# A linear-attention and sine-feed-forward kernel: mixed rows kept in order until the store, the head's copies dealt out anew, decay rates on another queue

## The chip, the cores and the metric

The kernel runs on one core of a Trainium2 chip. A core has five engines with queues of their own: TensorE (PE, matrix products from SBUF into PSUM banks), VectorE (DVE), ScalarE (ACT), GpSimd (POOL) and SyncE (SP, which here only issues transfers). Transfers between memory and SBUF run on 16 DMA engines; SP, ACT and POOL each have a queue to them. Engines run by themselves and wait for each other by semaphores. The metric is the device time of one execution in microseconds.

## The reference, cut to what matters

Stage one is linear attention with decay, for 4 batches, 8 heads, 768 positions, 64 channels; stage two is a feed-forward layer over the 3072 tokens of 512 channels:

```
for each block b of 64 positions:
    out[b] = ((q_b k_b^T) * lam^(i-j), lower triangle) v_b  +  (q_b * lam^(i+1)) state
    state  = lam^64 * state + (k_b * lam^(63-j))^T v_b
x   = out, tokens x 512
h   = x @ w_in                       # 512 -> 2048
g   = h + sin(alpha*h)^2 / (alpha + 1e-9)
res = g @ w_out                      # 2048 -> 512
```

## The kernel before, in words

**Tiling.** The kernel uses blocks of 128 positions, 24 in all (six to a batch), and gives tokens to stage two in six groups of 512 (four blocks). q and k are scaled by powers of the decay rate, cast to bf16 (`qk2`), transposed (`qkT`); a product of the two (S, L635) times a mask gives `Sm` (L646, DVE); `Sm` times v plus the earlier blocks' state times q gives the output piece O (L708, L721, L730), and k times v adds to the state Z (L671, copied to `Zd` or `Zc`). O lies in PSUM with channels on partitions and tokens along the columns, and is copied as columns of `xT` (L740). Stage two: unit A multiplies `w1` with `xT` (L779 for 512 columns, L813 for 256), ACT takes the sine (L789, L823), ACT or POOL the square (L793, L794, L827, L828), DVE makes `gT` (L796, L831); unit B multiplies `gT` with `w2` (L844), ACT copies it to `osb` (L857) and a transfer stores 128 tokens (L859).

**Mixed rows.** Blocks 0 to 3 are loaded in a shape that makes long runs: partition p of the q tile holds tokens 4p to 4p+3 (L357). After the transposes, column x of slot t is token 4x+t. The copy to `xT` (L740) puts the tokens back in order: it reads "t x" and writes "x t", so each write steps over `nq` columns, 4 in blocks 0 to 3 and 2 later, where pairs of blocks are loaded in the same way.

**Order.** A planner (`_Plan`) gets every operation with an engine, or a choice of engines, and a duration. It goes through time, gives each engine what is ready first (PE looks 40 operations ahead, SP takes its own in the order of the program), models the transfers, and writes each engine's instructions out in that order with the waits needed. Durations in it decide order and the choice of engine. `ported` marks operations that the planner keeps from running beside each other on DVE and POOL. Gaps of PE in the head are filled with matmuls on a constant tile (L935).

**The head.** Before stage two starts, SP issues the loads of q, k and v of blocks 0 to 3 and of the first quarter of `w1`; ACT requests the decay rates (`lam`, L426) and `alphaT` (L427). The rates go through Ln and Exp on ACT to the factors `Lq`, `Lp`, `Lk`. POOL issues the other weight loads (L346 from L397 and L418) between its own operations. The load of block 4's q waits until the third quarter of `w1` has landed (L901). The stores of the first 512 tokens are kept back and given to SP in one go (L960 to L962); in SP's order they stand behind the loads of blocks 10 and 11 and ahead of those of block 12. All other stores are issued by ACT, but the last one.

Of the kernel before, what the change touches and what calls it, by code (L numbers as in the profile page):

```python
# [6 lines left out]
ACTF = mybir.ActivationFunctionType  # L7
# [236 lines left out]
def bass_lightning_attn__then__act_snake_kernel(  # L244
# [31 lines left out]
    RO = 4  # L276
    RX = 3
    RU = 4
    QD = ((0, 0), (1, 0))

    es = contextlib.ExitStack()
    with es:
# [51 lines left out]
        def _(_unused_eng):  # L334
# [7 lines left out]
            def bank(i):  # L342
                return ("bank", i)
# [79 lines left out]
                )  # L423

            last = {}
            load(lam_bc[:, :], bass.AP(lam.tensor, 0, [[0, 128], [1, H]]), "lam", 0.1, "lam", "ACT", runs=1)  # L426
            load(alphaT[:, :], bass.AP(moe_alpha.tensor, 0, [[128, NM], [1, 128]]), "alphaT", 0.1, "alphaT", "ACT", lat=4.9, runs=1)  # L427
            load_q(0)
            load_kv(0, "k")
# [27 lines left out]
            for i in range(2):  # L457
                op("POOL", lambda e, i=i: e.memset(Zd[i][:, :, :], 0.0), 0.5, writes=[("Zd", i, 0), ("Zd", i, 1), "select"])

            op("ACT", lambda e: e.activation(lnlam[:, :], lam_bc[:, :], ACTF.Ln), 1.5, ["lam"], ["lnlam"])  # L460
            lnlam_b = bass.AP(lnlam, 0, [[H, 128], [0, 2 * NB + 4], [1, H]])
            op("DVE", lambda e: e.tensor_tensor(lnL[:, :, :], E_f[:, :, :], lnlam_b, ALU.mult), 0.2,
               ["E_f", "lnlam"], ["lnL"])
            op("ACT", lambda e: e.activation(Lq[:, NB:NB + 4, :], lnL[:, 2 * NB:2 * NB + 4, :], ACTF.Exp), 0.3,
               ["lnL"], ["Lq4"])
            op("ACT", lambda e: e.activation(Lp[:, :, :], lnL[:, 0:NP, :], ACTF.Exp, scale=-1.0), 0.2,
               ["lnL"], ["Lp"])
            op("ACT", lambda e: e.activation(Lk[:, :, :], lnL[:, NB:2 * NB, :], ACTF.Exp, scale=-1.0), 0.3,
               ["lnL"], ["Lk"])
            op("ACT", lambda e: e.activation(Lq[:, 0:NB, :], lnL[:, 0:NB, :], ACTF.Exp), 0.3, ["lnL"], ["Lq"])  # L470
            op("ACT", lambda e: e.activation(warm[:, :], lnlam[:, 0:1], ACTF.Sin, scale=0.0), 1.5,
               ["lnlam", "Lk", "Lq", "Lq4", "Lp"], ["warm"])

            op("PE", lambda e: e.transpose(ps[4][:, 0:NM], alphaT[:, :], identf[0:NM, 0:NM]), 0.3,
               ["alphaT", "identf"], [bank(4)])
            op("DVE", lambda e: e.tensor_copy(alpha[:, :], ps[4][:, 0:NM]), 0.2, [bank(4)], ["alpha"])
            op("DVE", lambda e: e.tensor_scalar_add(aeps[:, :], alpha[:, :], 1e-9), 0.2, ["alpha"], ["aeps"])
            op("DVE", lambda e: e.reciprocal(rinv[:, :], aeps[:, :]), 0.2, ["aeps"], ["rinv"])

            def QE(s, a):  # L480
                return "DVE" if (s, a) in QD else "POOL"

            def ported(o):
                o.port = True
                return o

            def scale_block(s):
                n, jl, j = s % NB, s % RL, s % R2
                lk = bass.AP(Lk, n * H, [[NB * H, 128], [1, H], [0, D]])
                jq = s // 2 % (RL // 2)  # L490
                if s == 0:
                    for a in range(2):
                        for t in (0, 2):
                            (op(QE(a, t),
                               lambda e, a=a, t=t: e.tensor_tensor(
                                   qk2[:, t:t + 2, 4 * a:4 * a + 4, :],
                                   bass.AP(q32, (a * H * 2 + t) * D,
                                           [[RL * H * D, 128], [D, 2], [4 * D, 4], [1, D]]),
                                   bass.AP(Lq, (NB + t) * H + 4 * a, [[(NB + 4) * H, 128], [H, 2], [1, 4], [0, D]]),
                                   ALU.mult),  # L500
                               1.05 if QE(a, t) == "POOL" else 0.9,
                               [("q32", a, 0), ("q32", a, 1), "Lq4"], [("q2", t, a), ("q2", t + 1, a)]))
                for a in range(2) if s % 2 == 0 and s > 2 else ():
                    ported(op("POOL",
                       lambda e, a=a: e.tensor_tensor(  # L505
                           qk2[:, j:j + 2, 4 * a:4 * a + 4, :],
                           q32[:, jq, 4 * a:4 * a + 4, :, :].rearrange("p h t d -> p t h d"),
                           bass.AP(Lq, n * H + 4 * a, [[(NB + 4) * H, 128], [H, 2], [1, 4], [0, D]]), ALU.mult),
                       1.05, [("q32", jq, a), "Lq"], [("q2", j, a), ("q2", j + 1, a)]))
                if s < NP:  # L510
                    for a in range(2) if s % 2 == 0 else ():
                        eng, dur = (("DVE", 0.9) if a == 0 else ("POOL", 1.05)) if s == 0 else ("POOL", 1.05)
                        (op(eng, lambda e, a=a: e.tensor_tensor(  # L513
                            qk2[:, j:j + 2, H + 4 * a:H + 4 * a + 4, :],
                            pair32(k32, jl, a).rearrange("p h t d -> p t h d"),
                            bass.AP(Lp, n * H + 4 * a, [[NP * H, 128], [H, 2], [1, 4], [0, D]]), ALU.mult),
                           dur, [("k32", jl + a), "Lp"], [("k2", j, a), ("k2", j + 1, a)]))
                    for a in range(2) if s % 2 == 0 else ():
                        op("ACT" if s + a == 0 else "POOL", lambda e, a=a: (e.copy if e is nc.scalar else e.tensor_copy)(
                            v2[:, j:j + 2, 4 * a:4 * a + 4, :],  # L520
                            pair32(v32, jl, a).rearrange("p h t d -> p t h d")), 0.62,
                           [("v32", jl + a)], [("v2", j, a), ("v2", j + 1, a)])
                    return
                ported(op("POOL",
                   lambda e: e.tensor_tensor(qk2[:, j, H:2 * H, :], block32(k32, jl), lk, ALU.mult), 1.05,  # L525
                   [("k32", jl), "Lk"], [("k2", j, 0), ("k2", j, 1)]))
                op((("ACT", 0.62, 0.0), ("POOL", 1.05, 0.3)) if s > 11 else "ACT",
                   lambda e: (e.copy if e is nc.scalar else e.tensor_copy)(v2[:, j, :, :], block32(v32, jl)), 0.62,  # L528
                   [("v32", jl)], [("v2", j, 0), ("v2", j, 1)])
# [94 lines left out]
            def part_S(s, b0, b1):  # L624
                jt = s % RT
                jq, nq, u = queries(s)

                def mm(e):
                    ins = None
                    for jp in range(4):  # L630
                        for h in range(2):
                            r = slice(64 * h, 64 * h + 64)
                            for c in range(2) if s < NP else (None,):
                                x = slice(0, 128) if c is None else slice(64 * c, 64 * c + 64)
                                ins = e.matmul(  # L635
                                    ps[(b0, b1)[h]][x, 128 * jp:128 * (jp + 1)].rearrange("p (t x) -> p t x", t=nq),
                                    qkT[r, jt, 4 + jp, x],
                                    qkT[r, jq:jq + nq, jp, u if c is None else queries(s // 2 * 2 + c)[2]],
                                )
                    return ins  # L640

                assert b1 == b0 + 1
                mi, js = (s % 2, s % 4) if s < NP else (2, s % 2)

                def then():
                    op("DVE", lambda e: e.tensor_tensor(  # L646
                        Sm[js][:, :, :],
                        banks[:, 512 * b0:512 * b0 + 1024].rearrange("p (c i) -> p c i", i=128),
                        bass.AP(mask[mi], 0, [[128, 128], [0, 8], [1, 128]]), ALU.mult), 1.25, [bank(b0), bank(b1), ("mask", mi)], [("Sm", js)])

                return mm, 0.33, [("qT", jq + t) for t in range(nq)] + [("kT", jt)], [bank(b0), bank(b1)], then

            def diag(s):
                return s < NP - 1 or s >= SD
# [37 lines left out]
            def part_O(s, ob, ob2=None):  # L692
# [43 lines left out]
                    return ins  # L736

                def then():
                  for eng, a0, a1, dur in ((("ACT", 0, 2, 0.45), ("DVE", 2, 4, 0.4)) if ob2 is not None else (("ACT" if s < 2 else (("ACT", 0.73, 0.4), ("DVE", 0.7, 0.0)), 0, 4, 0.74),)):
                    op(eng, lambda e, a0=a0, a1=a1: (e.copy if e is nc.scalar else e.tensor_copy)(  # L740
                        xT[c % RX][:, a0:a1, BL * i4:BL * (i4 + 1)].rearrange("p a (x t) -> p a t x", t=nq),
                        ps[obs[a0 // 2]][:, 128 * a0:128 * a1].rearrange("p (a t x) -> p a t x", a=a1 - a0, t=nq)), dur,
                       [bank(obs[a0 // 2])], [("xT", c % RX, i4, a) for a in range(a0, a1)])

# [92 lines left out]
            def unit_B(c, s4, mq, ob, lo=0, hi=DM, out_eng="ACT"):  # L837
# [18 lines left out]
                row = TCH * c + 128 * s4  # L856
                op("ACT", lambda e: e.copy(osb[jo][:, w], ps[ob][:, w]), 0.6, [bank(ob)], [("osb", jo)])  # L857
                def store(eng):
                    op(eng, lambda e: e.dma_start(out[row:row + 128, w], osb[jo][:, w]), 0.75,  # L859
                       [("osb", jo)], [], dma=f"out{jo}", issue=0.3, runs=8)  # L860

                if out_eng is None:
# [31 lines left out]
            piece_O(3, 2, 5)  # L894
            load_w1_first()
            cast_w1_first()
            for i in range(1, 4):
                load_w1(i, [last["v32", 1]])
            for i in range(4):
# [136 lines left out]
```

## Time and profile before

| | us |
|---|---|
| runs | 221.79, 222.25, 227.55 (median 222.25) |
| profiled execution | 221.06 |
| its span | 219.2 |
| PE busy | 207.6 (95%) |
| ACT, DVE, POOL busy | 157.2, 123.0, 96.0 |
| PE's first matmul of stage two (L813) | 20.58 |
| last load of q, k, v landed | about 122 |

Times within the profile count from the start of the span; 1.86 us of the profiled execution lie outside it. "Busy" is the time in which an engine has an instruction; PE's matmuls overlap, so a busy PE need not be at its peak. The slices of the page are 5.48 us each, a digit is a share in tenths. A line such as "ACT u L827" is an operation of ACT that writes tile `u` at line 827 of the kernel; "DMA q<-in_q_dram" is a transfer from its issue to its landing; "SPq" is SP at issuing.

### The profile page before, as it was taken

The numbers are of one execution on the slowest core, as the hardware profiler recorded it, in microseconds if no ns is written. First come the engines' busy times: TensorE is split into PE (matmuls) and PEld (weight loads), VectorE is DVE, ScalarE is ACT, GpSimd is POOL, SyncE is SP. The second block draws the span as 40 slices with busy tenths as digits, with TensorE's granted clock in tenths as the row PEclk, the third lists the DMA queues.
The fourth block names the chain that finished last, engine by engine and source line by source line (L and its number), as shares of the span: only waits on it lengthen the run. The fifth ranks groups of instructions, "written<-read, shape, count | busy, mean of one in ns | idle before, by whom it ended". The sixth has DMA issues, their size and how long they took to land.

```text
span 219.2 us, 4238 instructions
## 1 busy us (share of the span) xinstructions
PE 207.6 (95%) x1714; PEld 112.2 (51%) x1739; DVE 123.0 (56%) x185; ACT 157.2 (72%) x279; POOL 96.0 (44%) x110
## 2 busy tenths in 40 slices
PE   7787999999999979999999999999999999999995
PEld 2365544446577656555445444545544444444454
DVE  4688675444878858957564556545464544444100
ACT  4577986364988888969798787878778677777221
POOL 7793677756886777574551533011001011110100
PEclk9999999999999999999999999999999999999999
DMA  4999999999999999999999560110011011101212
GB/s 132 310 314 210 207 215 214 220 219 250 235 314 221 240 186 271 162 290 179 281 254 208 123 144 10 41 48 35 16 48 51 0 48 48 51 0 48 87 58 96
DMA packets 78499, 33.31 MB, mean 152 GB/s; under 512 B 55296, under 2 KB 75536, under 8 KB 78480
## 3 DMA queue, kind: packets, MB, share of 16 engines
q1 hardware_dynamic: 71728, 24.25, 53.4%
q0 software_dynamic: 3696, 3.67, 10.1%
q10 hardware_dynamic: 3056, 5.13, 6.5%
q8 instruction: 13, 0.21, 0.4%
q14 instruction: 6, 0.05, 0.1%
HBM read 27.28 MB, written 6.29 MB: 153 GB/s over the span
## 4 chain that ended last, share of the span: by engine, by line
PE 66%; DMA 20%; POOL 5%; ACT 3%; DVE 2%; issue 2%; SPq 1%; ACTq 0%; POOLq 0%
PE bank L844 33%; PE bank L779 22%; DMA k<-in_k_dram 10%; PE bank L813 4%; DMA w<-in_moe_w_in_dram 4%; DMA q<-in_q_dram 3%; DMA v<-in_v_dram 3%; PE bank L730 2%; PE bank L635 2%; POOL qk L513 2%; SPq L346 1%; POOL u L794 1%; POOL qk L505 1%; PE bank L708 1%; DVE gT L831 1%
## 5 line engine op out<-in xcount | busy, mean ns | idle before, releaser
L844 PE MATMUL bank<-w,gT 128*128 128x512 bf16 (+1 forms) x382 | 91.3, 371 | 1.8 <-issue 1.3
L796 DVE SCALAR_TENSOR_TENSOR gT<-u,rinv,bank 128x512 bf16<-128x512 bf16 x74 | 54.6, 745 | 52.2 <-ACT u L793 30.0
L779 PE MATMUL bank<-xT,w 128*128 128x512 bf16 x290 | 73.1, 379 | 0.6 <-issue 0.2
L789 ACT ACTIVATE t<-bank,alpha 128x512 bf16<-128x512 f32 x74 | 50.5, 686 | 23.2 <-PE bank L779 23.1
L794 POOL TENSOR_TENSOR u<-t 128x512 bf16<-128x512 bf16 x26 | 26.9, 1039 | 86.6 <-ACT t L789 84.7
L844 PEld LDWEIGHTS bank<-w,gT 128*128 128x128 bf16 x400 | 37.9, 98 | 39.5
L779 PEld LDWEIGHTS bank<-xT,w 128*128 128x128 bf16 x296 | 28.5, 98 | 34.1 <-ACT xT L740 0.6
L646 DVE TENSOR_TENSOR Sm<-bank,mask 128x1024 bf16<-128x1024 f32 x24 | 29.1, 1222 | 10.4 <-PE bank L671 7.1
L793 ACT ACTIVATE u<-t 128x512 bf16<-128x512 bf16 x48 | 30.0, 628 | 1.3
L857 ACT COPY osb<-bank 128x512 f32<-128x512 f32 (+1 forms) x25 | 14.2, 571 | 14.3 <-PE bank L844 14.2
L505 POOL TENSOR_TENSOR qk<-q,Lq 128x512 bf16<-128x512 f32 x20 | 20.4, 1042 | 8.2 <-DMA q<-in_q_dram 8.2
L813 PE MATMUL bank<-xT,w 128*128 128x256 bf16 x176 | 22.5, 273 | 1.5 <-DVE gT L831 1.5
L525 POOL TENSOR_TENSOR qk<-k,Lk 128x512 bf16<-128x512 f32 x20 | 20.8, 1042 | 2.6 <-DMA k<-in_k_dram 2.5
L823 ACT ACTIVATE t<-bank,alpha 128x256 bf16<-128x256 f32 x44 | 18.5, 474 | 4.5 <-PE bank L813 4.1
L831 DVE SCALAR_TENSOR_TENSOR gT<-u,rinv,bank 128x256 bf16<-128x256 bf16 x44 | 18.8, 474 | 4.9 <-ACT u L827 2.6
L813 PEld LDWEIGHTS bank<-xT,w 128*128 128x128 bf16 x176 | 16.1, 98 | 4.8 <-DVE gT L831 2.4
L740 ACT CAST xT<-bank 128x512 bf16<-128x512 f32 (+1 forms) x18 | 14.4, 799 | 3.6 <-PE bank L671 2.2
L528 ACT CAST v<-v 128x512 bf16<-128x512 f32 x16 | 9.8, 614 | 4.3 <-DMA v<-in_v_dram 4.3
L828 POOL TENSOR_TENSOR u<-t 128x512 bf16<-128x512 bf16 x9 | 9.3, 1038 | 6.5 <-ACT t L823 6.5
L730 PE MATMUL bank<-Sm,v 128*64 128x128 bf16 (+1 forms) x224 | 11.0, 224 | 0.6 <-DVE Sm L646 0.3
L635 PE MATMUL bank<-qkT 64*128 64x128 bf16 (+1 forms) x224 | 9.6, 219 | 0.3 <-ACT qkT L594 0.2
L935 PE MATMUL bank<-idle 128*128 128x512 bf16 x21 | 8.4, 540 | 1.6 <-DVE idle L441 1.5
(68 smaller groups left out, 125.7 us busy)
## 6 DMA issues: line engine op xcount, KB each, us to landing
q<-in_q_dram SPq DMA_DIRECT2D x12, 512.0 KB, 5.6
k<-in_k_dram SPq DMA_DIRECT2D x24, 256.0 KB, 5.5
v<-in_v_dram SPq DMA_DIRECT2D x24, 256.0 KB, 5.7
out_dram<-osb ACTq DMA_DIRECT2D x19, 256.0 KB, 2.0
w<-in_moe_w_out_dram POOLq DMA_DIRECT2D x4, 512.0 KB, 12.7
w<-in_moe_w_in_dram POOLq DMA_DIRECT2D x3, 512.0 KB, 8.0
ws<-in_moe_w_in_dram SPq DMA_DIRECT2D x2, 512.0 KB, 6.2
out_dram<-osb SPq DMA_DIRECT2D x4, 256.0 KB, 4.2
```

The source lines that it names most:

```text
L505: lambda e, a=a: e.tensor_tensor(qk2[:, j:j + 2, 4 * a:4 * a + 4, :], q32[:, jq, 4 * a:4 * a + 4, :, :].rearrange("p h t d -> p t h d"), b ...
L525: lambda e: e.tensor_tensor(qk2[:, j, H:2 * H, :], block32(k32, jl), lk, ALU.mult), 1.05,
L646: op("DVE", lambda e: e.tensor_tensor(Sm[js][:, :, :], banks[:, 512 * b0:512 * b0 + 1024].rearrange("p (c i) -> p c i", i=128), bass.AP(ma ...
L779: ins = e.matmul(ps[hb][:, c0:c1], w1[:, kc, 128 * m:128 * (m + 1)], xT[x][:, kc, c0:c1], start=(kc == 0 and c0 == lo), stop=(kc == NKC - ...
L789: op("ACT", lambda e: e.activation(t16[ju][:, w], ps[hb][:, w], ACTF.Sin, scale=alpha[:, m:m + 1]), 0.69 * f, [bank(hb), "alpha"], [("t16" ...
L793: lambda e: (e.activation(u16[ju][:, w], t16[ju][:, w], ACTF.Square) if e is nc.scalar else e.tensor_tensor(u16[ju][:, w], t16[ju][:, w], ...
L794: e.tensor_tensor(u16[ju][:, w], t16[ju][:, w], t16[ju][:, w], ALU.mult)), 0,
L796: op("DVE", lambda e: e.scalar_tensor_tensor(out=gT[g][:, m, w], in0=u16[ju][:, w], scalar=rinv[:, m:m + 1], in1=ps[hb][:, w], op0=ALU.mul ...
L813: ins = e.matmul(ps[hb][:, 256 * i:256 * i + 256], w1[:, kc, 128 * (m + i):128 * (m + i + 1)], xT[x][:, kc, lo:lo + 256], start=(kc == 0 a ...
L823: op("ACT", lambda e, i=i: e.activation(t16[ju][:, 256 * i:256 * i + 256], ps[hb][:, 256 * i:256 * i + 256], ACTF.Sin, scale=alpha[:, m + ...
L831: op("DVE", lambda e, i=i: e.scalar_tensor_tensor(out=gT[g][:, m + i, lo:lo + 256], in0=u16[ju][:, 256 * i:256 * i + 256], scalar=rinv[:, ...
L844: ins = e.matmul(ps[ob][:, w], gT[g][:, m, 128 * s4:128 * (s4 + 1)], w2[:, m, w], start=(m == 0), stop=(m == NM - 1),)
```

## The change

- The copy to `xT` of blocks 0 to 3 no longer reorders: it writes the columns as they come ("t x"). The tokens of the first group stay mixed within each block of 128 through stage two, which treats each token alone. The store of that group (c = 0) puts them back: its destination is 4 rows, stepping one token, of 32, stepping four tokens.
- `lam` is requested on SP, ahead of q, and no longer on ACT.
- The products with the decay factors: all four of q for blocks 0 to 3 on DVE (two were on POOL), three of the four of k on DVE (one was), one on POOL. They are marked `ported`. Three of four v copies are on POOL as before, but ACT has another one.
- `alpha` is copied out of PSUM by ACT in place of DVE; `aeps` and `rinv` come later in the program.
- Durations given to the planner change: Ln, Exp, S, and the copies to `xT` of blocks 0 and 1, which may now go to either ACT or DVE.

```
-    QD = ((0, 0), (1, 0))
+    QD = ((0, 0), (0, 2), (1, 0), (1, 2))
...
-            load(lam_bc[:, :], bass.AP(lam.tensor, 0, [[0, 128], [1, H]]), "lam", 0.1, "lam", "ACT", runs=1)
+            load(lam_bc[:, :], bass.AP(lam.tensor, 0, [[0, 128], [1, H]]), "lam", 0.1, "lam", "SP", lat=2.4, runs=1)
...
-            op("DVE", lambda e: e.tensor_copy(alpha[:, :], ps[4][:, 0:NM]), 0.2, [bank(4)], ["alpha"])
-            op("DVE", lambda e: e.tensor_scalar_add(aeps[:, :], alpha[:, :], 1e-9), 0.2, ["alpha"], ["aeps"])
-            op("DVE", lambda e: e.reciprocal(rinv[:, :], aeps[:, :]), 0.2, ["aeps"], ["rinv"])
+            op("ACT", lambda e: e.copy(alpha[:, :], ps[4][:, 0:NM]), 0.2, [bank(4)], ["alpha"])
...
-                        eng, dur = (("DVE", 0.9) if a == 0 else ("POOL", 1.05)) if s == 0 else ("POOL", 1.05)
-                        (op(eng, lambda e, a=a: e.tensor_tensor(
+                        eng, dur = ("DVE", 0.66) if s + a < 3 else ("POOL", 1.05)
+                        ported(op(eng, lambda e, a=a: e.tensor_tensor(
...
-                        op("ACT" if s + a == 0 else "POOL", lambda e, a=a: (e.copy if e is nc.scalar else e.tensor_copy)(
+                        op("ACT" if s and not a else "POOL", lambda e, a=a: (e.copy if e is nc.scalar else e.tensor_copy)(
...
-                        xT[c % RX][:, a0:a1, BL * i4:BL * (i4 + 1)].rearrange("p a (x t) -> p a t x", t=nq),
+                        xT[c % RX][:, a0:a1, BL * i4:BL * (i4 + 1)].rearrange(
+                            "p a (x t) -> p a t x" if s >= 4 else "p a (t x) -> p a t x", t=nq),
...
-                    op(eng, lambda e: e.dma_start(out[row:row + 128, w], osb[jo][:, w]), 0.75,
+                    rows = out[row:row + 128, w] if c else bass.AP(out.tensor, row * DM + lo, [[DM, 4], [4 * DM, 32], [1, hi - lo]])
+                    op(eng, lambda e: e.dma_start(rows, osb[jo][:, w]), 0.75,
                        [("osb", jo)], [], dma=f"out{jo}", issue=0.3, runs=8)
...
             cast_w1_first()
+            op("DVE", lambda e: e.tensor_scalar_add(aeps[:, :], alpha[:, :], 1e-9), 0.2, ["alpha"], ["aeps"])
+            op("DVE", lambda e: e.reciprocal(rinv[:, :], aeps[:, :]), 0.2, ["aeps"], ["rinv"])
```

More of the change, by code (lines that the diff above doesn't have):

```diff
@@ L458, in _ @@
                 op("POOL", lambda e, i=i: e.memset(Zd[i][:, :, :], 0.0), 0.5, writes=[("Zd", i, 0), ("Zd", i, 1), "select"])
-            op("ACT", lambda e: e.activation(lnlam[:, :], lam_bc[:, :], ACTF.Ln), 1.5, ["lam"], ["lnlam"])
+            op("ACT", lambda e: e.activation(lnlam[:, :], lam_bc[:, :], ACTF.Ln), 1.25, ["lam"], ["lnlam"])
             lnlam_b = bass.AP(lnlam, 0, [[H, 128], [0, 2 * NB + 4], [1, H]])
@@ L463, in _ @@
                ["E_f", "lnlam"], ["lnL"])
-            op("ACT", lambda e: e.activation(Lq[:, NB:NB + 4, :], lnL[:, 2 * NB:2 * NB + 4, :], ACTF.Exp), 0.3,
+            op("ACT", lambda e: e.activation(Lq[:, NB:NB + 4, :], lnL[:, 2 * NB:2 * NB + 4, :], ACTF.Exp), 0.2,
                ["lnL"], ["Lq4"])
@@ L469, in _ @@
                ["lnL"], ["Lk"])
-            op("ACT", lambda e: e.activation(Lq[:, 0:NB, :], lnL[:, 0:NB, :], ACTF.Exp), 0.3, ["lnL"], ["Lq"])
+            op("ACT", lambda e: e.activation(Lq[:, 0:NB, :], lnL[:, 0:NB, :], ACTF.Exp), 0.2, ["lnL"], ["Lq"])
             op("ACT", lambda e: e.activation(warm[:, :], lnlam[:, 0:1], ACTF.Sin, scale=0.0), 1.5,
@@ L493, in scale_block @@
                         for t in (0, 2):
-                            (op(QE(a, t),
+                            ported(op(QE(a, t),
                                lambda e, a=a, t=t: e.tensor_tensor(
@@ L500, in scale_block @@
                                    ALU.mult),
-                               1.05 if QE(a, t) == "POOL" else 0.9,
+                               1.05 if QE(a, t) == "POOL" else 0.66,
                                [("q32", a, 0), ("q32", a, 1), "Lq4"], [("q2", t, a), ("q2", t + 1, a)]))
@@ L649, in then @@
                         bass.AP(mask[mi], 0, [[128, 128], [0, 8], [1, 128]]), ALU.mult), 1.25, [bank(b0), bank(b1), ("mask", mi)], [("Sm", js)])
-                return mm, 0.33, [("qT", jq + t) for t in range(nq)] + [("kT", jt)], [bank(b0), bank(b1)], then
+                return mm, 0.25 if s < NP else 0.33, [("qT", jq + t) for t in range(nq)] + [("kT", jt)], [bank(b0), bank(b1)], then
             def diag(s):
@@ L738, in then @@
                 def then():
-                  for eng, a0, a1, dur in ((("ACT", 0, 2, 0.45), ("DVE", 2, 4, 0.4)) if ob2 is not None else (("ACT" if s < 2 else (("ACT", 0.73, 0.4), ("DVE", 0.7, 0.0)), 0, 4, 0.74),)):
+                  for eng, a0, a1, dur in ((("ACT", 0, 2, 0.45), ("DVE", 2, 4, 0.4)) if ob2 is not None else (((("ACT", 0.74, 0.0), ("DVE", 0.74, 0.8)) if s < 2 else (("ACT", 0.73, 0.4), ("DVE", 0.7, 0.0)), 0, 4, 0.74),)):
                     op(eng, lambda e, a0=a0, a1=a1: (e.copy if e is nc.scalar else e.tensor_copy)(
-                        xT[c % RX][:, a0:a1, BL * i4:BL * (i4 + 1)].rearrange("p a (x t) -> p a t x", t=nq),
+                        xT[c % RX][:, a0:a1, BL * i4:BL * (i4 + 1)].rearrange(
+                            "p a (x t) -> p a t x" if s >= 4 else "p a (t x) -> p a t x", t=nq),
                         ps[obs[a0 // 2]][:, 128 * a0:128 * a1].rearrange("p (a t x) -> p a t x", a=a1 - a0, t=nq)), dur,
```

## The prediction

> **What bounds the kernel now.** First the page: busy shares and the 40 slices.
>
> ```profile
> span 219.2 us, 4238 instructions
> ...
> PE   7787999999999979999999999999999999999995
> ...
> DMA  4999999999999999999999560110011011101212
> ```
>
> TensorE (PE) is full from slice 5 on, but for slice 14; the 16 DMA engines are full from slice 1 to 22 (5 to 123 us). So the first half has two limits. Which one holds, the chain of work shows, asked from 20 to 82 us (columns: start, length, what):
>
> ```profile
> 23.92 16.09 DMA k<-in_k_dram
> ...
> 62.26 6.40 DMA q<-in_q_dram
> ...
> 68.73 2.05 POOL qk L505 x2
> 70.78 0.58 SPq L346
> ...
> 71.40 6.17 DMA v<-in_v_dram
> ...
> 77.60 0.62 ACT v L528
> 78.21 0.54 ACT u L827
> ...
> 78.78 0.88 DVE gT L831 x2
> ...
> 79.71 1.05 PE bank L813 x8
> ```
>
> Twice PE waits for a landing: at 41.27 (0.48 us idle before it) for block 4's k, and at 79.71 (1.20 us idle) for a v cast that stands in ScalarE's (ACT's) order ahead of a square. After 79.71 PE has no gap over 0.2 us to the end. So whatever happens earlier, the time is the landing of that v (77.58) plus about 142 us. What sets that landing is the load queue of SyncE (SP), in its timeline:
>
> ```profile
> 58.29 1.05 SPq L346 DMA_DIRECT2D v<-in_v_dram  x1
> 59.39 2.83 SPq L859 DMA_DIRECT2D out_dram<-osb  x4
> 62.26 0.84 SPq L346 DMA_DIRECT2D q<-in_q_dram  x1
> ```
>
> Each issue begins within 0.06 us of the end of the last; so it goes from 39.84 to 79.96. The buffers that these loads overwrite were read 5 us or more before (block 6's q by 47.5, for the q load of 62.26), so SP waits for room behind transfers, not for PE; the chain's step from POOL to SP at 70.78 is inferred, and through q it would pass on the same delay. The four stores of the first 512 tokens stand in that queue directly ahead of the q load of the chain: there is no slack behind them.
>
> **The change, part by part.** Base: the profiled run, 221.06 us with 1.86 us outside its span.
>
> *Head, up to PE's first dense matmul (20.58).* Four of the eight products of q and k with the decay factors move from GpSimd (POOL) to VectorE (DVE): DVE now does four of q and three of k, POOL one of k. At 0.66 us (L495 on DVE) the seven take 4.6 us and end about 0.7 us after the third k lands (10.08), near 10.8 to 11.2; two qkT copies (0.42 us) follow, then the moved `aeps` and `rinv` (0.60 beside POOL's work and 0.25), then the four mask products, whose first began at 12.71. That gives 12.5 to 12.9: no gain there. `alpha` is now copied by ACT, and the bank of the first transposes waits for it; ACT is idle from 8.0 to 10.3, so it costs nothing; behind it stand only the qkT copies, which wait for q anyway.
>
> The contiguous copies do gain. The tile view of xT before 25 us gives 1308 ns median for 128x512 on ACT; later copies take
>
> ```profile
> L740 ACT CAST xT<-bank x18: 717/738/1320, 15.8 to 165.1; 128x512 bf16<-128x512 f32 x17, 128x256 bf16<-128x256 f32 x1
> ```
>
> so 0.57 us less each. Two of them stand on ACT ahead of the Zd copies that the third and fourth output pieces wait for, two halves end the stage: PE's dense work starts some 0.8 to 1.1 us earlier. That lead is worth nothing by itself: at 41.27 and at 79.71 PE waits for landings that it does not move. Bounds: 0 to -1.1; I take 0.
>
> *Lam on SP.* The request took 0.44 us on ACT; ahead of the first q on SP, with the 0.06 us between issues, it delays all later issues by 0.5 us. DMA is full from 4 us on, so the stream is late by that at 79.71. Bounds: 0 (lam's 4 KB only reach engines that are not full yet) to 1.1 (q's first packet, at 2.5 us in the trace, behind lam's last, at 3.6); I take the issue's +0.5. The decay rates need not land earlier for q, which itself lands at 5.8.
>
> *POOL's weight loads.* The second now follows the first directly (it was issued at 15.50, 2 us later). Issues stay ahead of the transfers, which run back to back at 185 to 208 GB/s from 17 to 27 us: nothing. The planner's other new durations leave PE's order after the head unchanged; one square and one v cast swap ACT and POOL late, 0.62 against 0.63 us: nothing.
>
> *The permuted store.* The four stores of tokens 0 to 511 wrote 128 rows one after another; now the destination is 4 rows of 32, and the outermost count falls from 128 to 4. Windows show what the stores cost:
>
> ```profile
> 56.00:62.00 6.00, 5.74 (x81) 4.03 (x81) 4.65 (x10) 5.86 (x15) 5.94 (x6) 1.00 1.21 248
> 62.50:64.50 2.00, 1.95 (x18) 1.44 (x17) 1.12 (x3) 1.98 (x5) 2.00 (x3) 1.00 1.09 412
> ```
>
> The last column is GB/s: 1.05 MB of stores at 412 take 2.5 us on all 16 engines. How a transfer is dealt to engines is to be had from packet counts. A lone later store has 144 packets (the DMA view, 135 to 140 us): 128 rows and 16 completions. The alphaT load, whose outermost count is 16, has 32 (4 to 6.2 us): 16 rows and 16 completions, each row with its own completion 23 ns behind it. So a share is whole rows of the outermost count. No transfer in the trace has an outermost count under 16. Bounds: shares as now, 0; four shares of 32 rows, one per outermost row: 103 GB/s, 10.2 us, **7.6 us more** on the four engines that carry them. Every load behind has its sixteenth on each of those engines and lands when the last arrives. I take +7.6, as the alphaT row is nearest.
>
> The Trainium skill, "DMA: Bandwidth & Descriptors", section "Why a DMA increments its semaphore by 16 and not by 1", has a rule for it: the engines are the largest number up to 16 that divides the slowest counts of both sides. By it this store gets 4 and the sum is the one below; by an even deal of rows it is 7.6 us less; the trace's packet counts agree with the rule and do not test it under 16.
>
> *What follows.* v would land at 77.58 + 0.5 + 7.6 = 85.7 and PE go on at 87.8 after some 9 us of idling. At the end of this trace the granted clock falls to 0.51 at 218.9, 2.3 us after the last matmul; at its start 5.8 us of matmuls (1.52 to 7.28) ran at half rate (631 ns median against 378) until the trace's first record of the full clock. So after the wait PE loses 0 to 2.9 us; I take the middle, +1.4.
>
> The Trainium skill, "TensorE: Matmul & The Clock Gate", Part 1, states windows of about 3.4 us both for losing and for regaining the clock. By that page the loss is an estimated 1.7 us, and the sum 0.3 us more.
>
> Sum: 221.06 + 0 + 0.5 + 7.6 + 1.4 = **230.6 us**. The runs shown have a median of 222.25, 1.2 above the profiled one; a median of the changed kernel may lie as much higher.
>
> **Rivals.**
>
> *Sixteen shares (not slower).* The store is dealt by rows whatever its counts. Its place is the store at 59.4; it decides at any split into 16. For it: 128 rows of 2 KB are as many as before. Against: alphaT's whole rows. Then the late stream (+0.5) and the absorbed lead are all: 221.06 + 0.5 = 221.6, within 220.5 to 222.6.
>
> *The lead survives (faster, by little).* If the stream starts no later and the store is dealt as before, and the loads behind 41 us gain with the earlier start, up to 0.8 us is kept: 220.3. Against it: the SP queue without pauses.
>
> *Copies not faster.* If contiguous writes stay at 1.31 us, PE's lead is lost; since it is absorbed, the forecast stays the same.
>
> Within the forecast, things can go part of the way. From 67 to 72 us the DMA share is 0.88 against 1.2 when full, so 1.3 us might be caught up, and the lead of 1.1 might count: 221.06 + 7.6 - 1.3 - 1.1 = 226.3. Upwards: 1.1 for lam, 2.9 for the clock, and, if SP's queue runs dry behind blocked engines, once more the 2.4 us from a store's issue (59.39) to its first packets (61.8): 235.1.
>
> **Chances.** Forecast (four shares) 0.80, its range 226 to 235; sixteen shares 0.16; lead survives 0.04. The range 226 to 235 leaves out the two rivals. A measurement of this kernel tells about 2% (4.4 us) from no change. Slower by more than that (over 225.5): 0.78, the forecast but for 0.02 in which still more is caught up; within 2%: 0.20, those 0.02, sixteen shares and half of the surviving lead; faster by more: 0.02, the other half, if the lead grows on the way.
>
> **What would show it.** Stores of the first 512 tokens that land 2 to 3 us apart instead of 0.6; about 8 us from their first packet during which DMA carries near 100 GB/s; an idle gap of PE of 8 us or more near 79 us behind a v cast on ACT, with the granted clock under 1 after it; k of block 4 landing at about 40.5; xT copies of 0.6 to 0.75 us and PE's first L813 matmul near 19.8. The prediction is wrong if the stores land as before (then 221.6), or if the gap comes but PE's work later than 80 us turns out to have had slack.

## The result and the profile after

The changed kernel takes **229.84 us** (median of its runs 229.08, 229.84 and 230.09) against 222.25 before: 1.034 times as long by these medians, and 1.032 by the estimate that has a 95% interval, 1.025 to 1.038. Ratios in this document leave out runs over 1.5% above the fastest of their kernel, here one of 355.58 us of the changed kernel (mean granted clock 0.56) and one of 358.71 us of the kernel before. The forecast was 230.6 us, range 226 to 235. The profiled execution took 229.84 us, its span is 228.1 us.

The page of the changed kernel, with the span and the 40 slices (each digit the busy share in tenths; PEclk is the granted clock):

```profile
span 228.1 us, 4261 instructions
...
PE   7887999999999907999999999999999999999995
...
PEclk9996799999999985999999999999999999999999
DMA  5999999999935799999999806101110111001122
```

Slices are counted from 0 and are 5.70 us each here. The hole of TensorE (PE) in slice 14 has become a whole empty slice. Ahead of it, in slices 11 to 13, the DMA engines, full before, carry a third to seven tenths. And the clock has two dents: one behind the hole, where the forecast has one, and one in slices 3 and 4, where it has none.

The chain of work, with the same steps that the prediction showed of before (start, length, what; these line numbers are up to 3 lower now):

```profile
63.55 0.47 SPq L858
...
64.07 12.61 DMA q<-in_q_dram
...
76.75 2.05 POOL qk L502 x2
78.80 0.63 SPq L346
...
79.47 5.51 DMA v<-in_v_dram
...
85.00 0.62 ACT v L525
...
87.11 1.89 PE bank L811 x8
89.00 1.49 PE bank L842 x4
```

It is the same chain. The q load behind the four stores takes 12.61 us instead of 6.40; the v of block 14 has landed at 84.98 instead of 77.58, and PE goes on at 87.11 instead of 79.71: 7.4 us later at both places. The four stores ahead of that q load were issued about 1 us later than the 59.39 of before, so up to 1 us of the delay of q is not the stores' own; what held the queue there stays open:

```profile
60.46 3.56 SPq L858 DMA_DIRECT2D out_dram<-osb  x4
```

The first group of matmuls behind the gate takes 1.89 us for what took 1.05: the granted clock there is 0.50, as a window shows (stretch, busy time of PE, PEld, DVE, ACT and POOL with counts, granted clock, DMA share, GB/s):

```profile
87.11:90.14 3.03, 3.02 (x12) 1.60 (x12) 1.86 (x3) 2.47 (x7) 2.44 (x3) 0.50 1.12 230
```

From there to the end PE has no wait over 0.2 us, as before.

The windows over the stores of the first 512 tokens, in the same columns:

```profile
62.00:64.50 2.50, 2.50 (x44) 2.14 (x39) 1.88 (x4) 2.43 (x7) 1.86 (x2) 1.00 0.56 123
64.50:67.00 2.50, 2.50 (x26) 1.71 (x26) 1.62 (x5) 1.88 (x5) 2.08 (x2) 1.00 0.28 101
```

101 GB/s at a DMA share of 0.28: a quarter of the 412 GB/s of before, on about a quarter of the engines.

What came out differently is the head. The timeline of PE, before and then after (start, length, matmuls; in brackets the idle time before):

```profile
19.25 0.24 PE L730 MATMUL bank<-Sm,v 64*64 64x128 bf16 x2 [0.23 <-issue]
...
20.58 2.02 PE L813 MATMUL bank<-xT,w 128*128 128x256 bf16 x16
```

```profile
18.80 0.31 PE L727 MATMUL bank<-Sm,v 64*64 64x128 bf16 x2 [1.18 <-issue]
...
20.58 3.60 PE L811 MATMUL bank<-xT,w 128*128 128x256 bf16 x16
```

PE's dense work begins at 20.58, to the hundredth where it began before, and its first 16 matmuls take 3.60 us instead of 2.02: the granted clock is 0.5 from 18.46 to 25.29.

### The profile page after: what moved, and what is told of

Same layout as the page of the kernel before. It is cut to its first block, busy times and chain, and to the rows that moved or that the text cites. A ratio compares the mean times of both kernels' runs of the same rounds, so it can differ in the third digit from the quotient of the medians.

```text
span 228.1 us, 4261 instructions
## 1 busy us (share of the span) xinstructions
PE 213.6 (94%) x1739; PEld 114.0 (50%) x1739; DVE 123.5 (54%) x188; ACT 156.0 (68%) x280; POOL 90.4 (40%) x106
## 4 chain that ended last, share of the span: by engine, by line
PE 79%; DMA 11%; DVE 3%; ACT 3%; SPq 2%; issue 1%; POOL 1%
PE bank L842 35%; PE bank L777 29%; PE bank L811 6%; DMA q<-in_q_dram 6%; PE bank L727 3%; DMA k<-in_k_dram 3%; DMA v<-in_v_dram 2%; PE bank L632 2%; DVE Sm L643 2%; SPq L346 1%; PE bank L705 1%; PE bank L668 1%; POOL qk L502 1%; DVE gT L829 1%; ACT xT L737 1%
## 5 line engine op out<-in xcount | busy, mean ns | idle before, releaser
L842 PE MATMUL bank<-w,gT 128*128 128x512 bf16 (+1 forms) x400 | 95.3, 373 | 0.0
L777 PE MATMUL bank<-xT,w 128*128 128x512 bf16 x296 | 74.5, 382 | 0.1
L792 POOL TENSOR_TENSOR u<-t 128x512 bf16<-128x512 bf16 x25 | 25.9, 1039 | 91.0 <-ACT t L787 85.6
L777 PEld LDWEIGHTS bank<-xT,w 128*128 128x128 bf16 x296 | 28.8, 99 | 34.6 <-issue 0.8
L811 PE MATMUL bank<-xT,w 128*128 128x256 bf16 x176 | 24.9, 293 | 7.2 <-DVE gT L829 7.2
L791 ACT ACTIVATE u<-t 128x512 bf16<-128x512 bf16 x49 | 30.6, 628 | 1.4
L855 ACT COPY osb<-bank 128x512 f32<-128x512 f32 (+1 forms) x25 | 14.2, 569 | 14.5 <-PE bank L842 14.2
L811 PEld LDWEIGHTS bank<-xT,w 128*128 128x128 bf16 x176 | 17.2, 104 | 11.5 <-DVE gT L829 8.2
L737 ACT CAST xT<-bank 128x512 bf16<-128x512 f32 (+1 forms) x18 | 12.5, 695 | 5.6 <-PE bank L727 3.4
L525 ACT CAST v<-v 128x512 bf16<-128x512 f32 x15 | 9.1, 613 | 7.2 <-DMA v<-in_v_dram 7.2
L826 POOL TENSOR_TENSOR u<-t 128x512 bf16<-128x512 bf16 x9 | 9.3, 1038 | 11.5 <-ACT t L821 11.5
L727 PE MATMUL bank<-Sm,v 128*64 128x128 bf16 (+1 forms) x224 | 11.5, 230 | 1.5 <-issue 1.2
L727 PEld LDWEIGHTS bank<-Sm,v 128*64 128x64 bf16 (+1 forms) x224 | 7.4, 112 | 4.2 <-issue 1.5
```

Source lines behind the costliest of these rows:

```text
L727: ins = e.matmul(ps[obs[jp // 2]][64 * h:64 * h + 64, 128 * jp:128 * (jp + 1)], v2[r, jj, 2 * jp + h, :], Sm[i][r, 4 * h + jp, :], start=( ...
L777: ins = e.matmul(ps[hb][:, c0:c1], w1[:, kc, 128 * m:128 * (m + 1)], xT[x][:, kc, c0:c1], start=(kc == 0 and c0 == lo), stop=(kc == NKC - ...
L791: lambda e: (e.activation(u16[ju][:, w], t16[ju][:, w], ACTF.Square) if e is nc.scalar else e.tensor_tensor(u16[ju][:, w], t16[ju][:, w], ...
L792: e.tensor_tensor(u16[ju][:, w], t16[ju][:, w], t16[ju][:, w], ALU.mult)), 0,
L811: ins = e.matmul(ps[hb][:, 256 * i:256 * i + 256], w1[:, kc, 128 * (m + i):128 * (m + i + 1)], xT[x][:, kc, lo:lo + 256], start=(kc == 0 a ...
L842: ins = e.matmul(ps[ob][:, w], gT[g][:, m, 128 * s4:128 * (s4 + 1)], w2[:, m, w], start=(m == 0), stop=(m == NM - 1),)
```

## Experiments

The theory (A): the destination of each permuted store has an outermost count of 4, so 4 of 16 DMA engines carry it, every load behind waits for those four, and the idle time costs PE its clock afterwards. Rivals: the head or lam's new place costs the time (B); rows 8 KB apart are slow by themselves (C); any outermost count under 16 falls to one fixed rate (D).

### The parts taken apart: e1_plain and e2_alone

`e1_plain` undoes only the contiguous columns and the permuted stores:

```diff
-  "p a (x t) -> p a t x" if s >= 4 else "p a (t x) -> p a t x", t=nq)
+  "p a (x t) -> p a t x", t=nq)
...
-  rows = out[row:row + 128, w] if c else bass.AP(out.tensor, row * DM + lo, [[DM, 4], [4 * DM, 32], [1, hi - lo]])
+  rows = out[row:row + 128, w]
```

> The changed kernel with its first part undone alone: the copies of blocks 0 to 3 interleave their columns again and the stores write 128 rows in order; the head as dealt out anew and lam on SyncE's queue stay. Theory A (the stores are carried by 4 DMA engines, and the idle time then costs the clock): the stores take 2.5 us, v at the gate lands at about 77, no drop of the clock near 83 us; 221 to 223 us, 0.960 to 0.970 of the changed kernel. Rival B (the 8.8 us come from the new head or from lam's place, with the stores slow as a consequence): 229 to 230. Two theories of the head's clock drop at 18.5 us: if it follows from the copies' speed, it is gone here, if from the rest of the new head, it stays.

`e2_alone` makes the same two edits alone, the other way round, in the kernel before.

> The kernel before with the first part alone: contiguous columns for blocks 0 to 3 and the permuted stores; lam on ScalarE's queue and the head as before. Theory A: +7.4 at the gate near 80 us, +1.4 for the clock after it, less what the earlier PE gains (nothing, PE waits): 229 to 231 us, 1.030 to 1.045 of the kernel before. Rival B: 221 to 223. If the head's clock drop at 18.5 us belongs to the new head, the clock is whole there in this run, PE idles some 8.5 us at 79 rather than 7.

Measured: `e1_plain` 221.79 us (221.18 to 223.58, 10 runs), `e2_alone` 231.37 us (230.21 to 234.32, 4 runs). The whole loss comes and goes with these two edits; B falls. `e2_alone` lies 0.4 us above its expected range. Which of the two edits it is, `e5_rows16` below tells. The chain of `e2_alone`:

```profile
64.04 12.39 DMA q<-in_q_dram
...
79.13 5.70 DMA v<-in_v_dram
...
86.97 1.89 PE bank L814 x8
```

These are the numbers of the changed kernel within 0.4 us, without lam on SyncE's (SP's) queue and without the new head. In `e1_plain` q takes 5.74 us and PE idles 1.37 us near 79 us.

The head's dent in the clock appears in both profiles, 3.41 us long, from 19.60 and from 20.21. So it needs neither the fast copies nor the new head; the expectation that one of the two would lose it was wrong.

### Engines or rows: e3_four, e5_rows16, e5_rows8, e5_rows2, e4_whole

`e3_four` sends each store as four transfers of 32 rows:

```diff
+  return [e.dma_start(bass.AP(out.tensor, (row + t) * DM + lo, [[4 * DM, 32], [1, hi - lo]]),
+                      osb[jo][32 * t:32 * t + 32, w]) for t in range(4)]
```

> The changed kernel with each permuted store cut into four transfers of 32 rows that stand 8 KB apart; the same rows go to the same places, but each transfer's outermost count is 32. Theory A (the outermost count sets the number of engines): 16 engines carry each, data at about 400 GB/s again; the price is 16 requests on SyncE instead of 4, at 0.4 us each (lam's request took that) 6.4 us against 2.8 before, of which the transfers still in flight cover 2.4 us: 221 to 225 us. Rival C (rows written 8 KB apart are slow by themselves, however many engines): 229 to 232.

Measured: 228.5 us (226.95 to 229.51), outside theory A's range and near C's. The timeline of SP and the page's list of DMA issues (KB each, us from issue to landing) say why:

```profile
59.10 9.68 SPq L861 DMA_DIRECT2D out_dram<-osb  x16
```

```profile
out_dram<-osb SPq DMA_DIRECT2D x16, 64.0 KB, 1.7
```

The 64 KB transfers land 1.7 us (median) after their request and do not pile up. But the 16 requests hold SP for 9.68 us, where 4 requests held it for 2.83 before: 0.6 us each instead of the 0.4 taken from lam's. So the loads behind come late again, now for want of requests; q's is issued at 68.82. The run does not tell A from C. The next ones do.

`e5_rows16`, `e5_rows8` and `e5_rows2` keep everything but the destination's counts:

```diff
-  [[DM, 4], [4 * DM, 32], [1, hi - lo]]
+  [[DM, 16], [16 * DM, 8], [1, hi - lo]]      # rows8: 8 and 16; rows2: 2 and 64
```

> The changed kernel with the destination of the four stores as 16 rows of 8 in place of 4 rows of 32; the rows of the first 512 tokens then stand in another order than the reference has, nothing else differs. Theory A (engines = outermost count): 16 engines, 2.5 us for 1.05 MB, no gate of 7 us: 220.5 to 222.5 us, 0.960 to 0.970 of the changed kernel. Rival C (any permuted write is slow): 229 to 231.

> The changed kernel with the destination of the four stores as 8 rows of 16 in place of 4 of 32 (the first 512 tokens' rows stand in another order than the reference's). Theory A (engines = outermost count): 8 engines, 206 GB/s, 5.1 us for 1.05 MB, 2.5 us more than with 16; the idle time of TensorE near 79 us is then some 4 us, about the 2.5 to 4.5 us after which the clock has fallen in the runs so far, so a fall of the clock may or may not come: 223.5 to 226.5 us. Theory D (anything under 16 falls to the rate of 4): 229 to 231.

> The changed kernel with the destination of the four stores as 2 rows of 64 (the first 512 tokens' rows in another order than the reference's). Theory A: 2 engines, 52 GB/s, 20.2 us, 17.7 us more than with 16 engines and 10 more than with 4; with the clock's loss 238 to 242 us. Theory D or any fixed price of the permuted form: 229 to 231.

Windows over the stores, of rows 2 and then of rows 8, each a stretch in which hardly anything but the stores moves (columns as above):

```profile
64.50:67.00 2.50, 2.50 (x30) 1.93 (x28) 2.50 (x5) 1.67 (x5) 1.58 (x2) 1.00 0.13 51
```

```profile
65.00:65.75 0.75, 0.75 (x11) 0.51 (x10) 0.75 (x3) 0.13 (x2) 0.75 (x1) 1.00 0.53 202
```

| outermost count | GB/s in a window over the stores | block 12's q landed | block 14's v landed | PE idle near 79 us | median, us |
|---|---|---|---|---|---|
| 2 | 51 | 84.38 | 92.90 | 16.46 | 239.36 |
| 4 (the change) | 101 | 76.68 | 84.98 | 6.97 | 229.84 |
| 8 | 202 | 71.67 | 80.34 | 3.53 | 225.8 |
| 16 | 304 (loads among them) | 68.56 | 78.68 | 1.86 | 221.95 |
| 128 (`e1_plain`) | 339 (loads among them) | 67.95 | 77.84 | 1.37 | 221.79 |

51 over 2, 101 over 4 and 202 over 8 are all 25 to 26 GB/s per unit of the outermost count. The DMA shares in the same windows, 0.13, 0.28 and 0.53, are 2.1, 4.5 and 8.5 of 16 engines, with a few packets of other transfers among them. That is A in its own numbers; C falls with 16 (rows 32 KB apart, no loss) and D with 8. With 16 the fast copies and the permuted rows are both there and the loss is not, so it is the outermost count that costs the time. The Trainium skill, "DMA: Bandwidth & Descriptors", section "Why a DMA increments its semaphore by 16 and not by 1", lets a transfer use the largest number of engines up to 16 that divides the slowest counts of both sides; by that rule these stores get 2, 4, 8 and 16, and the rates agree.

The landings of v are later than with 16 by 14.2, 6.3 and 1.7 us; those of q by 15.8, 8.1 and 3.1, so 1.4 to 1.8 us are caught up between q and v. The stores' own times, worked out from the rates, differ by 17.7, 7.6 and 2.5.

`e4_whole` keeps the contiguous copies and gets the outermost count back by its layout: column t times 128 plus p for token 4p+t.

```diff
-  bass.AP(out.tensor, row * DM + lo, [[DM, 4], [4 * DM, 32], [1, hi - lo]])
+  bass.AP(out.tensor, s4 * DM + lo, [[4 * DM, 128], [1, hi - lo]])
...
+  xT[c % RX][:, a0:a1, :].rearrange("p a (t i x) -> p a t i x", t=4, i=4)[:, :, :, i4, :]
```

> The changed kernel with the columns of all four mixed blocks laid out together: column t times 128 plus p for token 4p+t, so that the copies still write 32 columns in one piece, and each of the four stores takes one t and writes 128 rows that stand 8 KB apart; the first two units of the first product wait for all four blocks. The output is the reference's. Theory A (outermost count 128, 16 engines): no gate of 7 us, 220 to 222.5 us, 0.985 to 1.00 of the kernel before. Rival C (rows 8 KB apart are slow): 229 to 231.

Measured: 222.57 us (222.32 to 222.93, 12 runs), 0.9975 of the kernel before, interval 0.9941 to 1.0009. The permuted rows cost nothing that can be measured once 128 of them stand outermost. But the planner gave PE another order from 42 us on, with small waits (0.96 us at 83.3 the longest), and fast copies bring nothing that can be measured.

### Where the stores stand: e10_late_permuted and e9_late_stores

Both move the four stores behind block 14's v in SP's order, with everything else in the same order: the first those of the changed kernel, the second the plain ones of `e1_plain`.

```diff
+  late = [o for o in order if o.eng == "SP" and str(o.dma).startswith("out")][:4]
+  order = [o for o in order if o not in late]
+  order[at:at] = late          # at: behind the load of block 14's v
```

> The changed kernel with its four permuted stores (4 rows of 32) behind block 14's v in SyncE's order, everything else in the same order. They still take some 10 us on 4 engines, but the gate's loads no longer stand behind them. If only the place of the stores makes them dear: 220 to 222.5 us, 0.955 to 0.97 of the changed kernel. If the loads and the transposes behind block 14's v have less slack than 7.6 us: 223 to 229, with a wait of TensorE after 82 us instead of at 80.

Measured: 231.45 us (230.27 to 231.76), above both ranges. Block 14's v has landed at 74.86, and PE passes 80 us without a wait. But now the transposes and block 15's loads stand behind the stores, in the timeline of SP (a transpose there holds it for 7.59 us; the first one behind block 14's v held it for 3.31 before) and the chain:

```profile
74.96 7.59 SPq L535 DMA_TRANSPOSE qkT<-qk  x1
```

```profile
83.22 7.97 DMA v<-in_v_dram
...
93.83 1.89 PE bank L815 x8
```

PE idles from 85.37 to 93.83, 8.46 us, and loses its clock as before. It is not the place that makes four engines dear: what comes next in the queue has no slack either.

> The kernel e1_plain (stores of 128 rows in order, interleaved copies, new head, lam on SyncE's queue) with the four stores of the first 512 tokens behind block 14's v in SyncE's order instead of ahead of block 12's q; everything else in the same order. Theory A says that these stores cost what they do because the loads up to that v stand behind them: their 2.5 us leave the path, v lands near 75.3, TensorE's wait of 1.4 us near 79 us goes; 219.5 to 221.2 us, about 0.99 of the kernel before. If the loads behind block 14's v have no slack either, the wait comes back later: 221.5 to 223.

Measured: 220.87 us (219.80 to 221.80, 12 runs), 0.9948 of the kernel before, interval 0.9912 to 0.9983. v has landed at 74.31 and the wait at 79 us is gone; in the chain a shorter one comes back at block 15's v:

```profile
77.03 4.31 DMA v<-in_v_dram
...
83.97 1.05 PE bank L814 x8
```

0.73 us in place of 1.37. `e9_late_stores` is 0.9 us below `e1_plain`, from which it differs by the place of the stores alone, and so by little faster than both kernels.

### Lam: e6_lam_act, e7_lam_sp and e8_lam_second

`e6_lam_act` sends lam's request on ScalarE's (ACT's) queue again, in the changed kernel.

> The changed kernel with lam asked for on ScalarE's queue again; every other instruction in the same order. The prediction's term (lam on SyncE's queue delays each later load by 0.5 us): all landings 0.4 to 0.5 us earlier than in the changed kernel, first k at 7.4, block 4's k at 39.1. What the changed kernel's trace suggests instead (lam's request off ScalarE's queue sends q's first packets earlier): first q at 5.8, first k at 8.3, block 4's k at 40.0, 0.4 later. Time 229 to 231 by both, since later gates move with it by under 0.5.

Measured: 231.57 us (2 runs). Neither side was right: the first q has landed at 7.44 (5.40 in the changed kernel), the first k at 9.89 (7.92), block 4's k at 41.62 (39.55): about 2 us later, not 0.4 in one direction or the other; the time lies above the expected 229 to 231. ACT's timelines show lam's arrival, in the changed kernel and then in `e6_lam_act`:

```profile
3.95 0.21 ACT L460 ACTIVATE lnlam<-lam_bc 128x8 f32<-128x8 f32 x1 [1.40 <-DMA lam_bc<-in_lam_dram]
```

```profile
6.74 0.21 ACT L461 ACTIVATE lnlam<-lam_bc 128x8 f32<-128x8 f32 x1 [3.60 <-DMA lam_bc<-in_lam_dram]
```

In the trace of before, lam's packets ran from 1.86 and q's from 2.52. In `e6_lam_act` q's came first, at 1.92, and lam's at 3.06, though both requests were issued at 0.81 as before. So with two queues either can come first. The runs of the kernel before had hinted at two outcomes: of 59 timed beside these experiments, 24 lie between 221.2 and 222.6 us and 35 between 223.8 and 227.4, and none between. The clusters differ in the clock too: the mean granted clock is 0.98 or more in all 24 of the lower and under 0.98 in 24 of the 35 of the upper. Two experiments test it.

`e7_lam_sp` is the kernel before with lam alone moved to SP's queue:

```diff
-  load(lam_bc[:, :], bass.AP(lam.tensor, 0, [[0, 128], [1, H]]), "lam", 0.1, "lam", "ACT", runs=1)
+  op("ACT", lambda e: nc.sync.dma_start(lam_bc[:, :], bass.AP(lam.tensor, 0, [[0, 128], [1, H]])), 0.1,
+     dma="lam", lat=2.6, runs=1, writes=["lam"])      # planned as before, sent on SP
```

> The kernel before with lam asked for on SyncE's queue ahead of q, every other instruction in the same order. The timed runs of the kernel before fall in two clusters, 221.4 to 222.6 and 223.8 to 226.3 us. Theory L (with lam on ScalarE's queue, lam's packets and q's run for the same engines, and the upper cluster holds runs in which q's came first): only one cluster is left, 221.2 to 222.8 us, 0.985 to 0.995 of all runs of the kernel before. The prediction's term (+0.5 for the later requests): two clusters as before, 0.5 higher.

`e8_lam_second` is the kernel before with alphaT requested ahead of lam on ACT's queue.

> The kernel before with the two requests on ScalarE's queue exchanged, alphaT first and lam second, every other instruction in the same order. Theory L: q's packets are now always first, lam lands at about 6.7 us instead of 4.3 and the first q near 7.4: all runs in the upper cluster or above it, 223.8 to 227 us. Any other cause of the two clusters: both are there as before, or lam's 0.5 us later request moves both by up to 0.5.

Measured: `e7_lam_sp` has 11 of 12 runs between 220.74 and 222.64 and one at 224.03, median 221.8, beside 224.7 for the 23 runs of the kernel before taken with it (0.987). `e8_lam_second` has 225.14 to 227.0, all four runs in the upper cluster's range. There lam lands at 8.05, against the 6.7 expected and the 6.71 of `e6_lam_act`, and ACT waits still longer:

```profile
8.07 0.21 ACT L462 ACTIVATE lnlam<-lam_bc 128x8 f32<-128x8 f32 x1 [4.95 <-DMA lam_bc<-in_lam_dram]
```

PE's dense work then begins at 26.20 instead of 20.58, and the clock is 0.5 from 10.47 to 17.30 and from 24.13 to 30.95. So the upper cluster all but goes when lam alone is moved ahead of q, and comes back whole when lam is late; of all 56 runs of `e1_plain`, `e4_whole`, `e5_rows16`, `e7_lam_sp` and `e9_late_stores`, which have lam on SP, 4 lie above 223 us (223.58 to 224.18). That each run of the upper cluster is one in which q's packets came first is argued: no trace of such a run was taken, and in `e8_lam_second` lam is later than that alone would make it.

## Why the prediction was right, and where not

**The permuted store, +7.6: right.** The alphaT row had been the nearest one, and four shares was the answer. Measured are 101 GB/s (103 worked out), 8.0 us at the landing of block 12's q, against 8.1 forecast there with lam's term, and 7.4 at the gate; the difference was caught up in between. That the 8.1 was met so closely is in part luck: lam's 0.5 did not come, and the queue was 1 us late for another reason, which is open. The rival "sixteen shares" needed 412 GB/s.

**The clock, +1.4: right.** The clock is 0.5 from 83.32 to 90.14, and PE works in it from 87.11: 3.0 us at half rate, 1.5 lost. The profiles of the experiments put bounds on the term. PE worked at half rate behind the gap for 3.4 (`e5_rows8`, where the clock fell 0.95 us after PE had gone on), 4.7 (`e3_four`), 4.9 (`e2_alone`), 6.0 (`e5_rows2`) and 3.1 us (`e10_late_permuted`): losses of 1.5 to 3.0 us, so 1.4 was at the low end. That the middle of so wide a bound (0 to 2.9) came within 0.1 is luck; that the clock falls is not. But for those that the end of a trace cuts off, the half-clock stretches last 3.41, 6.83, 10.24 and 20.48 us, all multiples of 3.41. The Trainium skill, "TensorE: Matmul & The Clock Gate", Part 1, states windows of about 3.4 us; the traces agree with that length.

**The head, 0 at the end: right, and for another reason.** The copies are as fast as worked out (tile view of xT in the changed kernel, min/median/max in ns):

```profile
L737 ACT CAST xT<-bank x18: 373/722/753, 15.1 to 174.0; 128x512 bf16<-128x512 f32 x17, 128x256 bf16<-128x256 f32 x1
```

The mask products began at 12.04 instead of 12.5 to 12.9. The failed step is "PE's dense work starts some 0.8 to 1.1 us earlier": it started at 20.58 as before, because the matmuls of an output piece, 1.4 us ahead of before at 17.05, stopped for 1.18 us, and PE then ran at half rate to 25.29. At its wait for the gate (from 80.14) PE was 1.6 us later than before. The gate, 7.4 us later, took that in, as it would have taken the lead. Where the clock was whole there, the lead is seen to be absorbed as the prediction had it: in `e3_four` dense work began at 19.95 and PE waited 0.72 us at 40.06 for block 4's k.

**Lam on SP, +0.5: wrong in sign.** The step counted the request (0.40 us, as expected) and not what lam's packets do to q's. The first k landed at 7.92 instead of 8.27 and block 4's k at 39.55 instead of 40.01; at block 14's v little is left of it (77.29 in `e7_lam_sp`, 77.58 before). The bound "0 to 1.1" did not reach below nothing, and its upper end was misread: lam's last packet began at 3.99 in the trace of before, not at 3.6, which by the same working gives 1.5. Against the upper cluster of the kernel before (its median 224.92) the move is worth some 3 us, which the three runs of before hardly let one see.

The sum by the measured terms: 221.06 + 7.4 + 1.5 = 229.96 us; the profiled execution took 229.84. The terms missed by +0.5 for lam and +0.2 at the gate, less 0.1 for the clock: 0.6 of the 0.8 us by which the forecast stands above that execution; the rest is time outside the span and rounding.

## What to carry over

Before a store or load is permuted, look at the outermost count of its DRAM side: 2, 4 and 8 units carried some 25 GB/s each here, and 16 lost nothing that could be measured. With 4 instead of 128 the kernel lost 8 to 11 us at the two places where the stores were put. A copy of 1.3 us made 0.6 was worth nothing here, since the next landing gated the engine; the layout that keeps both (128 rows outermost) is the one to look for. A tiny load that the head waits for belongs ahead of the large ones in the same queue: with two queues it came first in some traces and last in another.

## What was not expected of the hardware

- Two requests issued at the same 0.81 us on two queues: in one trace lam's packets began at 1.86 and q's at 2.52, in another q's at 1.92 and lam's at 3.06. In the second lam landed 2.4 us later than in the first (6.71 against 4.34).
- The clock's first dent, at 18.5 to 20.5 us, needs no long idle time. It is there in the changed kernel, where PE's gaps over 0.15 us between 12 and 19 us were 0.66, 0.37 and 1.18 us. The dent came also in `e1_plain`, `e2_alone`, `e5_rows16`, `e5_rows2` and `e10_late_permuted`, and not in `e3_four`, `e4_whole`, `e5_rows8`, `e7_lam_sp` or `e9_late_stores`, though `e3_four` and `e4_whole` have the same three gaps. In `e6_lam_act` and `e8_lam_second`, where lam is late, the clock falls earlier, at 10.4 us. What decides it stays open.
- Near 18 us PE stops inside a group of 16 matmuls with nothing to wait for that the profile shows ("issue"): 0.23 us before, 1.18 in the changed kernel. A 16 KB packet of the instruction queue ends 1.3 us before the matmuls go on, in both (at 17.97 and 17.47). That the stop is a wait for instructions is argued and was not tested.
- Sixteen requests of 64 KB held SP for 9.68 us, four of 256 KB for 2.83.
